# Fewer and wider zero products, one table and one unit's decays moved on GpSimd, weights later on the queue, conversion steps placed by block

## The chip, the core and the metric

The kernel runs on one NeuronCore of a Trainium2 chip. Its engines are PE (TensorE: matrix products, with the weight loads PEld beside them), DVE (VectorE), ACT (ScalarE), POOL (GpSimd) and SP (SyncE, which here issues nearly all DMAs). The metric is the device time of one launch in microseconds.

## What is computed

The reference is retention, followed by two feed-forward blocks, all in float32:

```python
# q, k, v: 8 batches x 8 heads x 576 positions x 64
scores = scale * np.matmul(q, k.transpose(0, 1, 3, 2))
gamma = 1.0 - 2.0 ** (-5.0 - np.arange(H, dtype=np.float32))
Dmat = np.where(rel >= 0, gamma[:, None, None] ** rel[None, :, :], 0.0)   # rel = row - column
attn = np.matmul(scores * Dmat[None, :, :, :], v)
x = attn.transpose(0, 2, 1, 3).reshape(4608, 512)
h = np.maximum(np.maximum(x @ w1, x @ w2), x @ w3)        # 512 -> 768
x = h @ w_out                                             # 768 -> 512
h = x @ w_in                                              # 512 -> 2048
y = (h * np.clip(h + 3.0, 0.0, 6.0) / 6.0) @ w_out2       # 2048 -> 512
```

The weights come as float64 and are turned into float32 on the chip.

## The kernel before

**Units.** One batch and one pair of heads is a unit; there are 32. The first eight (batches 0 and 1, class `Summed`) open the kernel, and the loop over them is written out by hand: what each engine does, and in which order, is the order of the program, and every queue works in that order. A unit's q, k and v ("raw") are loaded by SP in two parts of 576 KB. `prepare` scales k by powers of gamma (on ACT and DVE or POOL for the first four, wholly on POOL for units 4 to 7, L365). `outers` (L382) and `scores` (L284) are its products; `copied` (ACT, L399), `join` (DVE, L416) or `carry` (PE, L405) form the running states; `mask` (DVE, L426) multiplies the scores by a table; `values_mm` (L320) multiplies by v; `values_rest` (DVE, L434) multiplies by a second table and calls `finish`, which splits the result into a high part (ACT, L333) and a low part (L336, a subtraction on POOL or DVE). Every float32 product of the feed-forward parts is three products of such parts: high by high, high by low, low by high (L525, L526, L527). The tables of the four pairs of heads are made by `fill` (DVE, L351). Units 2 to 6 put their subtraction on a list, `low`, that POOL works off from unit 5 on.

**Zeros.** Ahead of the first unit, PE multiplies zeros while the first loads are under way.

**Weights.** The first feed-forward part has 24 tiles of weights. Each goes through the class `Weights`, in the order `order_a`:

- `fetch`: SP loads 512 KB (L100) into one of three buffers `ws`;
- `begin`: two operations on DVE (L113, L114); `rise`: two on ACT (L121, L124);
- `join`: two on DVE (L132, L134), one product on POOL (L136), and then the `fetch` of a further tile, for which SP waits until a buffer is free;
- `end`: the high part by ACT (L147); `lows`: the low part by DVE (L153).

`step` calls, in this order: `end` for the oldest joined tile, `begin`, `rise`, `join` for the oldest tile that had begun before, `lows`. A block calls more steps if its own tile is not ended yet.

**Blocks.** A block (t, f, j) is 12 products: 512 tokens of tile t by weight j (of three) for the hidden slice f; (t, f) alone is the product with the output weights. With j = 0 ACT copies the sum out (L540), with j = 1 and 2 DVE takes the maximum (L542), and with j = 2 the result is split (L53 on ACT, L54 on DVE, the latter by a list that the next block works off). Two PSUM banks serve these sums in turn. Block (0, 0, 0) runs inside the loop, behind unit 6. The rest follows a list, `plan`: slot 0 is (0, 0, 0), slot 1 is (1, 0, 0), slot 2 (0, 0, 1), slot 3 (1, 0, 1), slot 4 (0, 0, 2), slot 5 (1, 0, 2), slot 6 (0, 1, 0) and so on; behind the six blocks of f >= 1 stands the output product (0, f - 1). Behind most slots stands a `step`. Ahead of slot 0's step ACT has `decay(8)`, which scales k of the ninth unit (L261). The ninth and tenth units' loads are issued by SP when the loop over the first eight has ended.

The later units ride along between the blocks, and the second feed-forward part follows; neither is touched.

Of the kernel before, what the change touches and what calls it, by code (L numbers as in the profile page):

```python
# [17 lines left out]
B, H, S, D = 8, 8, 576, 64  # L18
DM, FF1, FF2 = 512, 768, 2048
NT = B * S  # L20
C = 64
NC = S // C
HP = H // 2
KM = DM // P
F1, F2 = FF1 // P, FF2 // P
# [5 lines left out]
NA = 4 * F1  # L31
# [6 lines left out]
def retention_moe_moe2(ctx: ExitStack, tc, raw, w_a, w_b, factors, masks, out):  # L38
    nc = tc.nc
    gamma = [1.0 - 2.0 ** (-5.0 - h) for h in range(H)]  # L40

    def f32(ap):
        return ap.bitcast(F32)
# [28 lines left out]
    def x_tile():  # L72
        return x_pool.tile([P, 2, KM, TB], F32R, tag="x", name="x")

    def acc_tiles():
        return [ps_acc.tile([P, 512], F32, tag=f"o{m}", name=f"o{m}") for m in range(4)]
# [152 lines left out]
    wa = Weights(w_a, order_a, keep, nc.vector)  # L229
# [5 lines left out]
    halves = (slice(0, D), slice(D, P))  # L235

    def load_raw(i, room=None):
        if i >= len(units) or i in raws:
            return
        b, hp = units[i]  # L240
        t = room if room is not None else at.tile([P, RAW], F32, tag="raw", bufs=3, name="raw")
        raws[i] = t

        def part(c0, c1):
            nc.sync.dma_start(out=t[:, c0:c1], in_=raw[b, hp, :, c0:c1])

        if i:
            part(VS1, RAW)
            part(Z0, VS1)
            return  # L250
        part(VS1, VS0)
        part(VS0, RAW)
        part(Z0, VS1)

    def room():
        return rooms.tile([P, RAW], F32, tag="room", bufs=3, name="room")

    def decay(i):
        if i < len(units):
            k = raws[i][:, VS1:VS0]  # L260
            nc.scalar.mul(k, k, kdec_sb[:, units[i][1], NC:])  # L261

    xs, low = {}, []
    banks = [ps_at.tile([P, 512], F32, name=f"at{n}") for n in range(2)]

    class Unit:
# [63 lines left out]
        def finish(self, eng=None):  # L330
            b, hp, y = self.b, self.hp, self.y
            hi, lo = xs[b][:, 0, hp, :], xs[b][:, 1, hp, :]
            nc.scalar.copy(hi, y[:, :TB])  # L333

            def rest(eng):
                eng.tensor_tensor(out=lo, in0=y[:, :TB], in1=f32(hi), op=ALU.subtract)  # L336

            if eng is low:
                low.append(lambda: rest(nc.gpsimd))
            elif eng is not None:  # L340
                rest(eng)
            else:
                late.append(lambda: rest(nc.vector))
                late.append(lambda: nc.sync.dma_start(out=xe_d[:, hp, b * C:(b + 1) * C], in_=y[:, TB:]))
# [3 lines left out]
    def fill(hp):  # L348

        for n, one in enumerate((mask_sb, qdec_sb)):  # L350
            nc.vector.tensor_tensor(  # L351
                out=tables[hp][:, n].rearrange("p (c s) -> p c s", s=C),
                in0=one[:, hp, None, :].to_broadcast([P, NC - 1, C]),
                in1=powers_sb[:, hp, n, :NC - 1, None].to_broadcast([P, NC - 1, C]), op=ALU.mult)

    class Summed(Unit):
# [75 lines left out]
        def values_rest(self):  # L432
            self.y = (rooms if self.hp % 2 else at).tile([P, S], F32, tag="yr", bufs=2, name="yr")
            nc.vector.tensor_tensor(  # L434
                out=self.y[:, :TB], in0=self.ps[1], in1=tables[self.hp][:, 1], op=ALU.mult)
            self.finish(nc.gpsimd if self.i < 2 else low if self.i < 2 * HP - 1 else nc.vector)

        def put_end(self):
            t = raws[self.i].rearrange("p (k s) -> p k s", s=S)
# [91 lines left out]
    def up(t, f, j):  # L531
        x = xs[t]
        ps = ps_mm.tile([P, 512], F32, tag="mm", name="mm")
        for kk in range(KM):
            product(ps, wa_sb[3 * f + j], slice(kk * P, (kk + 1) * P),
                    (x[:, 0, kk, :], x[:, 1, kk, :]), kk == 0, kk == KM - 1)
        flush()
        if j == 0:
            tmp[t, f] = moe.tile([P, TB], F32, tag="t", bufs=3, name="t")
            nc.scalar.copy(tmp[t, f], ps)  # L540
            return
        nc.vector.tensor_tensor(out=tmp[t, f], in0=ps, in1=tmp[t, f], op=ALU.max)  # L542
        if j == 2:
            h = hid[t, f] = moe.tile([P, 2, TB], F32R, tag="hy", bufs=7, name="h")
            split(tmp.pop((t, f)), h[:, 0, :], h[:, 1, :])

    def down(t, f):

        flush()
        if f == 0:  # L550
            acc[t] = acc_tiles()
        h = hid.pop((t, f))
        for m in range(KM):
            product(acc[t][m], wa_sb[3 * F1 + f], slice(m * P, (m + 1) * P),
                    (h[:, 0, :], h[:, 1, :]), f == 0, f == F1 - 1)
            if f == F1 - 1:
                flush()
                if m % 2 == 0:
                    y = f32(pair())
                nc.scalar.copy(y[:, m % 2, :], acc[t][m])  # L560
                if m % 2:
                    late.append(lambda m=m, y=y: nc.sync.dma_start(out=x2_d[t][:, m - 1:m + 1, :], in_=y))
# [10 lines left out]
    with tc.manual_schedule():  # L573

        zeros = stage.tile([P, C], F32, bufs=1, name="zeros")
# [4 lines left out]
        load_raw(1)  # L580
        load_raw(2, room())
        load_raw(3, room())
        wa.fetch(1)
        load_raw(4, room())
        wa.fetch(1)
        load_raw(5)
# [4 lines left out]
        spare = acc_tiles()  # L591
        pairs = [banks, spare[:2], spare[2:],
                 [ps_mm.tile([P, 512], F32, tag="mm", name="mm") for n in range(2)]]
        us = [Summed(i, pairs[i % HP if i < 2 * HP - 1 else 0]) for i in range(2 * HP)]
        for n in range(40):
            nc.tensor.matmul(spare[3][halves[n % 2], :C], lhsT=zeros[halves[n % 2], :], rhs=zeros[halves[n % 2], :],
                             start=True, stop=True)
        us[0].prepare()
        fill(0)
        fill(1)  # L600
        us[0].outers()
        us[0].all_scores()
        us[0].copied(0)
        us[1].prepare()
        us[0].join()
        us[0].mask()
        us[1].outers()
        us[0].values_mm()
        us[1].all_scores()
        us[1].copied(0)  # L610
        fill(2)
        us[2].prepare()
        us[0].values_rest()
        us[1].mask()
        us[1].join()
        fill(3)

        def block(t, f, j=None):

            k = order_a.index(3 * F1 + f if j is None else 3 * f + j)  # L620
            while wa.ended < k + 1:
                wa.step()
            if j is None:
                down(t, f)
            else:
                up(t, f, j)


        for i, u in enumerate(us):
            one, two, three = (us[i + n] if i + n < len(us) else None for n in (1, 2, 3))  # L630
            if i:
                u.values_mm()
            u.put_end()
            if i == 0:
                load_raw(6)
            if i == 2:
                load_raw(7, room())
                wa.fetch(1)
            if one and one.i >= HP:
                one.carry()  # L640
            if three:
                three.prepare()
            if i == 0:
                ends.fill()
            if two:
                two.outers(True)
            if i:
                u.values_rest()
            begun, parts = wa.begun, wa.end() if i in (4, 6) else []
            if 1 < i < 6:  # L650
                wa.begin() if i != 4 else None
                if wa.joined < begun:
                    wa.join()
            wa.lows(parts)
            if two:
                two.copied(0)
                wa.rise()
                two.mask()
                if two.i < HP:
                    two.join()  # L660
            if i >= HP + 1:
                for n in range(2 if i < 2 * HP - 1 else len(low)):
                    low.pop(0)()
            if i == 2 * HP - 2:
                block(0, 0, 0)
        load_raw(8)
        load_raw(9)
        rooms.release()
# [10 lines left out]
        plan += [(0, f, 0), (1, f, 0), (0, f, 1), (1, f, 1), (0, f, 2), (0, f - 1), (0, f), (1, f, 2)]  # L679
        plan += [(1, g) for g in range(f)]  # L680
        decay(2 * HP)
        base = 2 * HP
        side = {(1, 1, 1): [(lambda k: ends.scores(), 0)], (1, 2, 0): [(lambda k: ends.values(), 0)],
                (1, f, 0): [(visit, 0)], (0, f, 1): [(ready, 0)], (1, f, 1): [(rest, 0)]}
        for n, (a, b) in enumerate(zip([(0, f - 1), (1, f, 2), (1, 1), (1, 3)], [(0, f), (1, 0), (1, 2), (1, 4)])):
# [2 lines left out]
        for n, blk in enumerate(plan):  # L688
            if n:
                block(*blk)  # L690
            if wa.ended < NA and n % 3 != 1 and blk != (1, 1, 1):
                wa.step()
                if wa.ended == NA - 1:
                    wb.fetch(2)
            if blk == (0, f, 2):
                xs[2] = x_tile()
            for act, k in side.get(blk, ()):
                act(base + k)
# [325 lines left out]
```

## Time and profile before

| | |
|---|---|
| median of 3 runs | 1457.69 us (1457.62 to 1459.07) |
| profiled execution, its own time | 1459.42 us |
| its span, first to last instruction | 1457.6 us |
| PE busy | 1442.6 us |
| DVE, ACT, POOL busy | 894.7, 448.2, 163.4 us |
[...]

In the rows below, a line of the timeline gives the start and the duration in us, engine, line of the kernel, operation, what it writes and reads, the number of instructions, and in brackets how long the engine was idle before it and who released it. "issue" is a wait for which the profile shows no releaser. A line of the table by stretches gives the stretch, its length, then busy us and instructions of each engine named, the granted clock of PE, the share of the DMA engines and GB/s. In the DMA lists the last number is the time from issue to landing.

### The profile page before, as it was taken

Reading aid. Unit: us, or ns where it says so; the run is one execution under the profiler, and the core shown is the slowest. Engines: PE = TensorE matmul, PEld = TensorE weight load, DVE = VectorE, ACT = ScalarE, POOL = GpSimd, SP = SyncE. Lnnn points to the kernel's source line nnn. Section 1 sums busy time; section 2 is a strip of 40 time slices with the busy share of each in tenths; the row PEclk is TensorE's granted clock in tenths of the full one; section 3 lists DMA queues with packets and bytes.
Section 4 is the critical chain, followed back from the end, with each engine's and each line's share of the span. In section 5 each row is a group of like instructions: output and inputs, shape, how many; then the busy total and the mean of one; then the engine's idle time right before and its main releaser. Section 6 shows DMA issues by size and latency. Waiting matters only on the chain.

```text
span 1457.6 us, 24529 instructions
## 1 busy us (share of the span) xinstructions
PE 1442.6 (99%) x9760; PEld 1248.5 (86%) x9760; DVE 894.7 (61%) x1851; ACT 448.2 (31%) x838; POOL 163.4 (11%) x124
## 2 busy tenths in 40 slices
PE   8999999999999999999999999999999999999998
PEld 7887888888888888888898899899898898898897
DVE  7888878777778752214446646555654655566544
ACT  5544233434343311112222322232232222223222
POOL 4434013333333300000000000000000000000000
PEclk9999999999999999999999999999999999999999
DMA  8434345656565501064643363364445436444431
GB/s 341 155 108 145 134 145 195 224 205 233 198 224 193 199 9 57 2 215 139 224 128 112 117 210 115 101 224 116 116 146 179 116 87 239 116 115 167 116 101 44
DMA packets 94402, 219.02 MB, mean 150 GB/s; under 512 B 14032, under 2 KB 17232, under 8 KB 94288
## 3 DMA queue, kind: packets, MB, share of 16 engines
q1 hardware_dynamic: 93920, 216.96, 45.2%
q8 instruction: 78, 1.28, 0.4%
q10 hardware_dynamic: 368, 0.48, 0.1%
q14 instruction: 36, 0.29, 0.1%
HBM read 174.42 MB, written 42.99 MB: 149 GB/s over the span
## 4 chain that ended last, share of the span: by engine, by line
PE 92%; DVE 5%; ACT 1%; issue 1%; DMA 0%; POOL 0%; ACTq 0%; DVEq 0%; POOLq 0%
PE mm L525 18%; PE mm L527 17%; PE mm L526 17%; PE o L865 5%; PE o L866 5%; PE o L864 5%; PE o L525 3%; PE o L527 3%; PE o L526 3%; PE p L866 3%; PE p L865 3%; PE p L864 3%; PE mm L320 2%; PE at L284 1%; DVE xf L755 1%; DVE g L821 1%
## 5 line engine op out<-in xcount | busy, mean ns | idle before, releaser
L53 ACT CAST gp<-g 128x384 fp32r<-128x384 f32 x192 | 98.6, 513 | 336.5 <-DVE g L821 334.0
L525 PE MATMUL mm<-x,w 128*128 128x512 f32 x468 | 184.6, 394 | 0.1
L527 PE MATMUL mm<-x,w 128*128 128x512 f32 x468 | 182.6, 390 | 0.2
L526 PE MATMUL mm<-x,w 128*128 128x512 f32 x468 | 182.3, 389 | 0.0
L54 DVE TENSOR_TENSOR gp<-g,gp 128x384 fp32r<-128x384 f32 x192 | 107.2, 558 | 112.0 <-ACT gp L53 112.0
L828 DVE TENSOR_TENSOR cc<-mm,c 128x384 f32<-128x384 f32 x142 | 78.7, 554 | 137.2 <-PE mm L527 95.4
L542 DVE TENSOR_TENSOR t<-mm,t 128x512 f32<-128x512 f32 x108 | 74.1, 686 | 136.6 <-PE mm L527 136.5
L865 PE MATMUL o<-w,gp 128*128 128x512 f32 x384 | 151.1, 394 | 0.0
L866 PE MATMUL o<-w,gp 128*128 128x512 f32 x384 | 150.5, 392 | 0.0
L864 PE MATMUL o<-w,gp 128*128 128x512 f32 x384 | 150.1, 391 | 0.0
L525 PE MATMUL mm<-T,wq 128*128 128x384 f32 x382 | 129.6, 339 | 0.9
L833 ACT COPY c<-mm 128x384 f32<-128x384 f32 x143 | 68.5, 479 | 197.1 <-PE mm L527 197.1
L527 PE MATMUL mm<-T,wq 128*128 128x384 f32 x382 | 128.8, 337 | 0.0
L526 PE MATMUL mm<-T,wq 128*128 128x384 f32 x382 | 128.5, 336 | 0.0
L136 POOL TENSOR_TENSOR wf<-wf,wp 128x512 f32<-128x512 f32 x56 | 83.3, 1489 | 317.3 <-DVE wp L134 300.0
L525 PEld LDWEIGHTS mm<-x,w 128*128 128x128 f32 x468 | 87.8, 188 | 19.7 <-DVE t L542 0.5
L527 PEld LDWEIGHTS mm<-x,w 128*128 128x128 f32 x468 | 87.8, 188 | 19.5 <-DVE w L153 1.0
L526 PEld LDWEIGHTS mm<-x,w 128*128 128x128 f32 x468 | 87.9, 188 | 17.9 <-DVE x L336 0.2
L53 ACT CAST h<-t 128x512 fp32r<-128x512 f32 x54 | 33.6, 622 | 205.5 <-DVE t L542 199.9
L525 PE MATMUL mm<-B,wq 128*128 128x384 f32 x286 | 96.4, 337 | 0.0
L527 PE MATMUL mm<-B,wq 128*128 128x384 f32 x286 | 96.3, 337 | 0.0
L526 PE MATMUL mm<-B,wq 128*128 128x384 f32 x286 | 96.1, 336 | 0.0
(182 smaller groups left out, 2917.9 us busy)
## 6 DMA issues: line engine op xcount, KB each, us to landing
wq<-wqd SPq DMA_DIRECT2D x336, 256.0 KB, 3.1
raw<-in_raw SPq DMA_DIRECT2D x55, 576.0 KB, 5.4
ws<-in_w_b SPq DMA_DIRECT2D x32, 512.0 KB, 4.8
ws<-in_w_a SPq DMA_DIRECT2D x24, 512.0 KB, 3.5
wqd<-y SPq DMA_DIRECT2D x24, 512.0 KB, 2.7
x2d<-y SPq DMA_DIRECT2D x18, 512.0 KB, 3.4
wod<-y SPq DMA_DIRECT2D x16, 512.0 KB, 3.2
w<-wod SPq DMA_DIRECT2D x16, 512.0 KB, 4.4
```

The costliest lines, as they stand in the source:

```text
L53: nc.scalar.copy(hi, full)
L54: late.append(lambda: nc.vector.tensor_tensor(out=lo, in0=full, in1=f32(hi), op=ALU.subtract))
L136: nc.gpsimd.tensor_tensor(out=frac, in0=frac, in1=f32(power), op=ALU.mult)
L525: nc.tensor.matmul(ps, lhsT=wh, rhs=xh, start=first, stop=False, skip_group_check=read)
L526: nc.tensor.matmul(ps, lhsT=wh, rhs=xl, start=False, stop=False, skip_group_check=read)
L527: nc.tensor.matmul(ps, lhsT=wl, rhs=xh, start=False, stop=last, skip_group_check=read)
L542: nc.vector.tensor_tensor(out=tmp[t, f], in0=ps, in1=tmp[t, f], op=ALU.max)
L828: nc.vector.tensor_tensor(out=c, in0=a, in1=b, op=ALU.add)
L833: nc.scalar.copy(c, ps)
L864: nc.tensor.matmul(outs[s], lhsT=gh, rhs=wo[f][:, 0, :], start=start, stop=False)
L865: nc.tensor.matmul(outs[s], lhsT=gh, rhs=wo[f][:, 1, :], start=False, stop=False)
L866: nc.tensor.matmul(outs[s], lhsT=gl, rhs=wo[f][:, 0, :], start=False, stop=stop)
```

## The change

1. The zero products become six, each 512 columns wide, instead of forty of 64.
2. `fill` makes the table of the last pair of heads on POOL instead of DVE, and the call moves ahead of unit 0's join.
3. The list `low` goes: units 0 to 6 call their subtraction on POOL at once.
4. One load of weights moves from behind unit 3's load to behind unit 7's; there are again three before the first join.
5. Unit 7's `prepare` moves from the loop's fifth round to its fourth.
6. The steps inside the loop are written out: tile 0 is begun in the fourth round (behind unit 5's mask), joined in the fifth, ended in the sixth, where tile 1 is begun; tile 1 is joined behind block (0, 0, 0).
7. In the plan a step stands behind every block but those of t = 1 with j = 0 or 2, and (1, 1, 1); before, it stood behind two slots of three.

```diff
@@ finish
-            if eng is low:
-                low.append(lambda: rest(nc.gpsimd))
-            elif eng is not None:
+            if eng is not None:
                 rest(eng)
@@ fill
-            nc.vector.tensor_tensor(
+            (nc.vector if hp < HP - 1 else nc.gpsimd).tensor_tensor(
@@ values_rest
-            self.finish(nc.gpsimd if self.i < 2 else low if self.i < 2 * HP - 1 else nc.vector)
+            self.finish(nc.gpsimd if self.i < 2 * HP - 1 else nc.vector)
@@ first loads
         load_raw(3, room())
-        wa.fetch(1)
         load_raw(4, room())
         wa.fetch(1)
         load_raw(5)
@@ zeros
-        for n in range(40):
-            nc.tensor.matmul(spare[3][halves[n % 2], :C], lhsT=zeros[halves[n % 2], :], rhs=zeros[halves[n % 2], :],
-                             start=True, stop=True)
+        for n in range(6):
+            own = halves[n % 2]
+            nc.tensor.matmul(spare[3][own, :].rearrange("p (n d) -> p n d", d=C), lhsT=zeros[own, :],
+                             rhs=zeros[own, None, :].to_broadcast([D, 512 // C, C]), start=True, stop=True)
@@ first units
         us[1].prepare()
+        fill(3)
         us[0].join()
...
         us[1].join()
-        fill(3)
@@ loop over the eight units
                 load_raw(7, room())
-                wa.fetch(1)
+                wa.fetch(2)
...
-            if three:
+            if three and i < HP:
                 three.prepare()
+            if i == HP - 1:
+                us[2 * HP - 1].prepare()
...
-            begun, parts = wa.begun, wa.end() if i in (4, 6) else []
-            if 1 < i < 6:
-                wa.begin() if i != 4 else None
-                if wa.joined < begun:
-                    wa.join()
-            wa.lows(parts)
             if two:
                 two.copied(0)
-                wa.rise()
                 two.mask()
                 if two.i < HP:
                     two.join()
-            if i >= HP + 1:
-                for n in range(2 if i < 2 * HP - 1 else len(low)):
-                    low.pop(0)()
+            if i == HP - 1:
+                wa.begin()
+                wa.rise()
+            if i == HP:
+                wa.join()
+            if i == HP + 1:
+                parts = wa.end()
+                wa.begin()
+                wa.rise()
+                wa.lows(parts)
             if i == 2 * HP - 2:
                 block(0, 0, 0)
+                wa.join()
@@ plan
-        base = 2 * HP
+        base, calm = 2 * HP, [(1, g, j) for g in range(F1) for j in (0, 2)] + [(1, 1, 1)]
...
-            if wa.ended < NA and n % 3 != 1 and blk != (1, 1, 1):
+            if wa.ended < NA and blk not in calm:
                 wa.step()
```

## Rows read from the trace of the kernel before

**Rows 1.** The page, busy time of each engine.

```profile
PE 1442.6 (99%) x9760; PEld 1248.5 (86%) x9760; DVE 894.7 (61%) x1851; ACT 448.2 (31%) x838; POOL 163.4 (11%) x124
```

**Rows 2.** Table by stretches, PE alone (busy us, instructions, clock, DMA share, GB/s).

```profile
5.52:40.66 35.14, 31.04 (x753) 0.95 0.93 362
30.00:35.00 5.00, 4.28 (x81) 0.66 0.45 140
40.66:140.00 99.34, 97.54 (x505) 1.00 0.38 118
```

**Rows 3.** Timeline of PE, 0 to 40 us.

```profile
0.98 3.99 PE L596 MATMUL o<-zeros 64*64 64x64 f32 x80 [0.98 <-DVE rebias L587]
5.52 2.17 PE L382 MATMUL at<-raw 64*64 64x256 f32 x26 [0.55 <-ACT raw L373]
...
24.45 0.27 PE L284 MATMUL at<-room 64*64 64x64 f32 x2 [1.12 <-issue]
...
30.72 1.03 PE L320 MATMUL at<-room 128*64 128x64 f32 x25 [1.90 <-issue]
```

**Rows 4.** The page's DMA queues; table by stretches, PE, PEld, DVE, ACT, POOL.

```profile
q8 instruction: 78, 1.28, 0.4%
...
18.26:24.45 6.19, 4.80 (x127) 3.92 (x127) 5.82 (x12) 2.28 (x5) 3.00 (x3) 1.00 1.02 407
```

**Rows 5.** Timelines of DVE, PE and POOL, 16 to 41 us.

```profile
16.04 1.70 DVE L351 TENSOR_TENSOR w<-masks_sb,factors_sb 128x512 f32<-128x512 f32 x2
...
20.18 1.15 PE L320 MATMUL o<-room 128*64 128x64 f32 x32 [0.28 <-DVE room L416]
...
35.08 5.85 POOL L336 TENSOR_TENSOR x<-yr,x 128x512 fp32r<-128x512 f32 x4
```

**Rows 6.** Timeline of SP, 23 to 38 us; DMA issues, 33.7 to 34.5 us.

```profile
23.43 10.70 SPq L100 DMA_DIRECT2D ws<-in_w_a  x3
34.18 3.51 SPq L245 DMA_DIRECT2D raw<-in_raw  x4
...
ws<-in_w_a SPq DMA_DIRECT2D x1, 512.0 KB, 3.4
...
raw<-in_raw SPq DMA_DIRECT2D x1, 576.0 KB, 4.5
```

**Rows 7.** Timeline of DVE, 39 to 58 us.

```profile
39.82 1.41 DVE L426 TENSOR_TENSOR room<-at,w 64x512 f32<-64x512 f32 x2
41.26 0.69 DVE L434 TENSOR_TENSOR yr<-o,w 128x512 f32<-128x512 f32 x1
...
50.49 0.69 DVE L542 TENSOR_TENSOR t<-mm,t 128x512 f32<-128x512 f32 x1 [1.69 <-PE mm L527]
51.10 0.42 DVE L113 TENSOR_SCALAR wp<-ws 128x512 uint32<-128x512 uint32 x1
...
52.37 0.69 DVE L134 SCALAR_TENSOR_TENSOR wp<-ws,wp 128x512 uint32<-128x512 uint32 x1
52.98 0.68 DVE L153 TENSOR_TENSOR w<-wf,w 128x512 fp32r<-128x512 f32 x1
...
56.56 0.68 DVE L153 TENSOR_TENSOR w<-wf,w 128x512 fp32r<-128x512 f32 x1
```

**Rows 8.** Timeline of ACT, 46 to 56 us.

```profile
46.11 0.77 ACT L261 ACTIVATE raw<-raw,factors_sb 128x576 f32<-128x576 f32 x1
...
54.85 0.62 ACT L147 CAST w<-wf 128x512 fp32r<-128x512 f32 x1 [2.05 <-POOL wf L136]
```

**Rows 9.** Timeline of PE, 47 to 54 us.

```profile
47.55 0.40 PE L525 MATMUL mm<-x,w 128*128 128x512 f32 x1
...
53.71 0.50 PE L527 MATMUL mm<-x,w 128*128 128x512 f32 x1
```

**Rows 10.** Timelines of POOL and PE, 123 to 130 us.

```profile
123.45 4.72 POOL L136 TENSOR_TENSOR wf<-wf,wp 128x512 f32<-128x512 f32 x2 [4.55 <-DVE wp L134]
...
129.24 0.50 PE L525 MATMUL mm<-x,v 128*128 128x512 f32 x1 [1.56 <-ACT t L540]
```

More of the change, by code (lines that the diff above doesn't have):

```diff
@@ L261, in decay @@
             nc.scalar.mul(k, k, kdec_sb[:, units[i][1], NC:])
-    xs, low = {}, []
+    xs = {}
     banks = [ps_at.tile([P, 512], F32, name=f"at{n}") for n in range(2)]
```

## The prediction

> **What bounds the kernel now.** I read the page's busy shares first: PE is busy 99% of the span [rows 1], so only its idle time and its slow clock can be won, and anything that makes it wait is lost in full. Then the busy time of PE by stretches. From the first real product to the first block of the feed-forward part (5.52 to 40.66) it idles 35.14 - 31.04 = 4.1 us, and the mean granted clock is 0.95; from there to 140 us it idles 1.8 of 99 us at full clock [rows 2]. [...] So the stretch that the change touches first holds 4.1 + 1.7 = 5.8 us at most. Third, the timeline of PE: two waits carry the releaser "issue", 1.12 us at 24.45 and 1.90 us at 30.72 [rows 3]: no engine and no data is late there, so the instructions themselves are. The clock falls just behind the second of them. Last, from 40.66 on, the conversion of the weights runs beside the blocks; I read DVE, ScalarE, the issues of SP and their landings there.
>
> **Why instructions are late.** The page's DMA part shows 78 packets of instructions on one queue, 1.28 MB, that is 16.4 KB each; PE and its weight loads record 2 x 9760, some 250 a packet [rows 1, 4]. Between 18.26 and 24.45 stand 127 + 127 records, in 6.2 us with the DMA engines at 1.02 of their time [rows 4], and from 24.45 to the wait that ends at 30.72 it is 6.3 us again [rows 3]. So while the loads fill the queues, PE gets some 256 instructions every 6.2 us.
>
> **The early part of the change.** The 40 small zero products are 80 records and 80 weight loads in 3.99 us [rows 3]; six wide ones are 12 + 12, 136 fewer. Their columns are 6 x 512 = 3072 against 40 x 64 = 2560, so by columns they take 3.99 x 1.2 = 4.8 us, from 0.98 to 5.8, where the first real product stood at 5.52: +0.25 us (ends 0, if the clock rises at the same time and the pairs overlap better, and 0.6). The 136 missing records move every boundary of the instruction packets 136 records further into the work. But each packet is also asked for that much later, 136/254 x 6.2 = 3.3 us, so the pace stays. The packets that came at 18.26 and 24.45 now come at some 21.4 and 27.7 and serve points 136 records on; the third, with the load queue emptying around 31, at some 33.5 instead of 34. Counted off PE's timeline, work alone gets to these points at 20.4, then 25.9 and 32.1, each from the packet before and less the waits of before. That is waits of 1.0, 1.7 and 1.4, 4.1 us. Before lost 1.12 + 1.90, 1.7 by clock [rows 2, 3] and 0.28 to a late join [rows 5]. 4.1 - 5.0 is -0.9, with the zeros **-0.7 us**; ends -5.8 (all of it comes back) and +1.5 (one of the new waits lets the clock fall too).
>
> [...]
>
> The fourth table (fill(3)) leaves DVE, 1.70 us at 16.04, for GpSimd [rows 5]. That brings the mask and join of unit 2 forward, on which PE waited 0.28 us at 20.18 [rows 5]; it is in the walk above. On GpSimd the two products are as wide as its subtractions, of which four took 5.85 us [rows 5]: 2.9 us behind the decays of unit 1, in a stretch where it waits for loads. The subtractions of units 2 to 6 lose their queue "low" and follow their unit; those four ran in a row from 35.08 to 40.93 [rows 5], PE waited for none, and will for none. Unit 7's decays one unit earlier on GpSimd wait for their load with only subtractions behind them; nothing of PE's. These I cost at nothing; their cover is GpSimd's idle time, and if it goes, the first block waits for x.
>
> **Weights later.** One load of weights goes behind unit 4's, one behind unit 7's. The early loads come 512 KB earlier, and go unnoticed by a PE that waits for instructions. What matters is who stands behind the weights on SP. The loads of weights 3 and 4 need the buffers that the joins of weights 0 and 1 free: three such loads took SP from 23.43 to 34.13, and the loads of raw 8 and 9 stand behind them, issued from 34.18 on, right after the second join [rows 6]. **The change moves the join of weight 1 from unit 4 to behind the first block**, and so raw 8 with it. On DVE its two operations (0.69 us each, [rows 7]) now follow, after the masks of unit 7 (1.41), a begin (2 x 0.42), weight 0's subtraction (0.68) and unit 6's product (0.69). The masks could start at 39.1, when PE's scores are there; 39.1 + 1.4 + 0.85 + 0.7 + 0.7 + 1.35 is 44.1. Before, that product ended at 41.95 [rows 7], so the earliest is 43.3; one block by GpSimd makes it 45.4. The next load of weights is issued there, and raw 8 behind it: 34.18 + 4.5 against 33.8, when the weights before it were issued and took 3.4 us to land [rows 6], is 4.9 us to landing. So raw 8 lands at 49.0. ScalarE has its decay (L261, 0.77 us) ahead of weight 1's copy (L147, 0.62) [rows 8]: at 50.4 the copy is done. Block (0,0,1), slot 2 of the plan, wants it at 47.55 [rows 9]: PE waits 2.85 us, and 0.25 more for DVE's subtraction behind the copy. **+3.1 us**, ends 2.1 and 4.4 + 0.25. Everything here is on the clock of before; an earlier PE shifts all of it alike.
>
> **Steps tied to blocks.** I wrote out begin, join and end for each slot, old and new. Before, weight 2 was joined in the step behind slot 0 and ended behind slot 2. Now it is joined behind slot 2 and ended behind slot 3, right ahead of slot 4, block (0,0,2), that needs it. Before ran just these operations at just this place, for weight 3: behind slot 2's maximum (L542 at 50.49) a begin, the join, GpSimd's product, ScalarE's copy at 54.85 to 55.47, and DVE's subtraction at 56.56 to 57.24 [rows 7, 8]. Slot 4's third product, the first to need the subtraction, stood at 53.71, just behind weight 2's subtraction at 52.98 to 53.66 [rows 7, 9]. So weight 2 comes a whole step later: 57.24 - 53.66 = 3.6 us. Slot 2's step has no subtraction of its own any more, which takes some 0.3 off: **+3.3 us** (ends 3.6, and 2.0, where only the copy is late and GpSimd's product isn't held up). What is late next is weight 3 at slot 6, 0.3 us by the same walk, inside these ends; from slot 13 on the new order is level with the old.
>
> **Clock.** In slot 4 PE is idle for some 1.9 us, works on two products, and is idle for 1.5 again. Behind 1.90 us of waiting the clock fell [rows 2, 3]; behind 1.56 us at 129.24 [rows 10] it did not. I take one such fall, **+1.7 us**; ends 0 and 3.4 (slot 2 as well).
>
> **Sum.** -0.7 + 3.1 + 3.3 + 1.7 = +7.4 us. The profiled execution took 1459.42 us with a span of 1457.6, so it would be 1466.8 with a span of 1465.0. Its own time is 1.7 us above the median of the runs, 1457.69; on the median the forecast is **1465.1 us**.
>
> **Rivals.** *Supply comes back whole (faster).* With 136 records fewer and weights out of the queue, packets might be asked for early enough. Then the early 5.8 us and the 0.55 before the first product [rows 3] return, 6.3. It decides from the point where the waits of slots 2 and 4 cost less than 3.4 together (6.3 less the 2.9 of the measurement), that is if one of them is covered; with slot 4 alone at its lower end, 2.0, it is 1457.7 - 6.3 + 2.0 = 1453.4. For it: two "issue" waits lie just at those boundaries. Against: the pace of 6.2 us is the queues', and the order of SP, ScalarE and DVE is fixed by the program. *Even.* Supply gives 5.8 and the waits cost 6.4: 1458.3. *Dearer.* A step behind the last part of the output product and one behind the next (0,f,0) follow without a DVE operation on PSUM between. Before has such a pair once: GpSimd's L136 x2 took 4.72 us from 123.45 while DVE ran on, ScalarE's copy was late, and PE waited 1.56 us at 129.24 [rows 10]. The new order has the pair at slots 12, 19 and 26, two more. With 2 x 1.56 and a second fall of the clock: +4.8, 1469.6. *The early part does nothing*: the waits for instructions end where they ended, whatever the number of records; the early term is 0 and the time 1465.8, inside the forecast.
>
> **How the numbers follow.** The measurement can tell about 0.2%, 2.9 us, from no change. Forecast (1460.6 to 1468.5) 0.52; dearer 0.18; even 0.18; faster 0.12. Below 1454.8 lies the last alone: faster 0.12, same 0.18, slower 0.70. The sum of all low ends is -5.8 + 2.1 + 2.0 = -1.7, that of the high ends 1.5 + 4.65 + 3.6 + 3.4 = +13.2; with the faster case partly inside, the range is 1455.5 to 1471.
>
> **What would show it.** Right: "issue" waits still 6.2 us apart with a full queue; the first raw load of 8 issued behind a join near 44 us; PE waiting for ScalarE's L147 ahead of slot 2 by 2 to 4 us, and at slot 4 for L147 and then L153; half clock behind it. Wrong: no "issue" wait after 20 us and full clock to 40; or slot 2 and 4 starting back to back; then the early term or the order that I wrote out is at fault.

## The result, and the profile after

The changed kernel took 1474.34 us (median of 5 runs, 1473.77 to 1475.43), the kernel before beside it 1459.07 (5 runs, 1457.62 to 1460.03): a ratio of 1.0108, 95% interval 1.0094 to 1.0123. It is slower, as forecast, but by 15 us where 7.4 were forecast: 1474.3 against 1465.1, above the range's end of 1471. The profiled execution took 1475.31 us with a span of 1473.3, which is 15.9 above the profiled execution before.

From 150 us on both traces run alike, so all of it lies ahead of that. The table gives the start of the first product of some slots, before and after; the last column is what was lost since the row above.

| slot | before | after | behind | lost since |
|---|---|---|---|---|
| 0, block (0, 0, 0) | 40.66 | 39.23 | -1.43 | -1.43 |
| 2 | 47.55 | 48.68 | +1.13 | 2.56 |
| 4 | 53.02 | 56.62 | +3.60 | 2.47 |
| 9 | 66.99 | 74.02 | +7.03 | 3.43 |
| 13 | 79.18 | 87.65 | +8.46 | 1.43 |
| 14 | 82.29 | 94.22 | +11.93 | 3.47 |
| 25 | 113.92 | 126.72 | +12.80 | 0.87 |
| 30 | 129.24 | 143.47 | +14.23 | 1.43 |
| 32, and from there on | 134.83 | 150.66 | +15.84 | 1.61 |

At slot 9 the kernel stands where the forecast had it for good, 7.0 against 7.4. Most of what is missing comes behind it, at slots 13 and 30. (The kernel before has 1.56 us of waiting of its own at slot 30, so the last rows show only what the changed kernel adds there.) The timeline of PE, 0 to 144 us, the zeros, the first product and then the lines with the long waits:

```profile
0.98 4.67 PE L594 MATMUL o<-zeros 64*64 64x512 f32 x12 [0.98 <-DVE rebias L584]
5.50 2.17 PE L380 MATMUL at<-raw 64*64 64x256 f32 x26
...
15.92 0.32 PE L380 MATMUL o<-room 64*64 64x128 f32 x1 [0.24 <-issue]
22.24 0.68 PE L320 MATMUL o<-room 128*64 128x64 f32 x15 [1.70 <-issue]
32.84 0.21 PE L284 MATMUL o<-raw 64*64 64x64 f32 x1 [1.25 <-issue]
...
48.68 0.50 PE L523 MATMUL mm<-x,w 128*128 128x512 f32 x1 [1.66 <-ACT w L147]
...
56.62 0.50 PE L523 MATMUL mm<-x,w 128*128 128x512 f32 x1 [1.93 <-ACT w L147]
...
58.39 0.50 PE L525 MATMUL mm<-x,w 128*128 128x512 f32 x1 [1.04 <-DVE w L153]
...
87.65 0.50 PE L523 MATMUL mm<-x,w 128*128 128x512 f32 x1 [0.86 <-ACT w L147]
...
90.33 0.80 PE L525 MATMUL mm<-x,w 128*128 128x512 f32 x1 [1.95 <-DVE w L153]
...
143.47 0.50 PE L523 MATMUL mm<-x,v 128*128 128x512 f32 x1 [2.65 <-ACT t L538]
```

(L523 to L525 are the three products, L525 to L527 before; L538 and L540 are the copy and the maximum, L540 and L542 before.) The first five lines answer to [rows 3], slot 2 to [rows 9], slot 30 to [rows 10]. In the kernel before slots 2, 4 and 13 start without a wait. Here a weight is late at each of them: its high part (L147), and at slots 4 and 13 then its low part (L153) too. The table by stretches (length, then busy us of PE, PEld, DVE, ACT and POOL with instructions, granted clock, DMA share, GB/s) shows what followed:

```profile
5.52:39.23 33.71, 29.66 (x755) 25.64 (x753) 25.23 (x41) 18.93 (x53) 18.71 (x18) 1.00 0.81 317
...
56.62:63.00 6.38, 5.34 (x15) 3.98 (x16) 2.48 (x5) 1.13 (x3) 1.66 (x1) 0.73 0.41 139
...
87.65:94.00 6.35, 4.40 (x12) 3.19 (x13) 5.58 (x10) 1.24 (x2) 2.22 (x2) 0.73 0.30 83
...
143.47:150.00 6.53, 6.53 (x22) 5.23 (x23) 4.55 (x11) 3.25 (x6) 1.27 (x1) 0.74 0.27 84
```

Three times the granted clock fell from 1.00 to 0.50 for part of a stretch (0.50 from 60 to 62, from 91 to 93 and from 145 to 148 us), each time behind waits: (1 - 0.73) x 6.38 = 1.7 us of work at 56.62, 1.7 again at 87.65 and at 143.47. The fall of [rows 2], ahead of 40 us, is not there.

**Slot 2.** The timelines of SP at 42 us and of ACT at 47 us:

```profile
42.21 0.33 SPq L100 DMA_DIRECT2D ws<-in_w_a  x1
42.59 0.42 SPq L245 DMA_DIRECT2D raw<-in_raw  x1
...
47.35 0.77 ACT L261 ACTIVATE raw<-raw,factors_sb 128x576 f32<-128x576 f32 x1 [1.84 <-DMA raw<-in_raw]
48.03 0.60 ACT L147 CAST w<-wf 128x512 fp32r<-128x512 f32 x1
```

The load of raw 8 stands behind the weight that the join of weight 1 let through, ACT's decay waits for it, and the copy of weight 1 stands behind the decay: the chain of the forecast, 1.7 us earlier than reckoned.

**Slot 13.** The timelines of DVE and ACT ahead of it:

```profile
84.05 1.77 DVE L54 TENSOR_TENSOR h<-t,h 128x512 fp32r<-128x512 f32 x1
85.74 0.68 DVE L540 TENSOR_TENSOR t<-mm,t 128x512 f32<-128x512 f32 x1
...
86.45 0.62 ACT L53 CAST h<-t 128x512 fp32r<-128x512 f32 x1 [2.48 <-DVE t L540]
86.98 0.61 ACT L147 CAST w<-wf 128x512 fp32r<-128x512 f32 x1
...
87.11 0.69 DVE L54 TENSOR_TENSOR h<-t,h 128x512 fp32r<-128x512 f32 x1 [0.69 <-ACT h L53]
87.71 0.42 DVE L113 TENSOR_SCALAR wp<-ws 128x512 uint32<-128x512 uint32 x1
...
89.59 0.69 DVE L153 TENSOR_TENSOR w<-wf,w 128x512 fp32r<-128x512 f32 x1
```

Slot 13, block (0, 2, 0), multiplies weight 7, and the new order ends weight 7 in the step behind slot 12, right ahead of it (before, behind slot 11). The copy on ACT waits behind L53 and so for the maximum; on DVE the subtraction (L153) stands last in its step, behind the low part of h (L54) and four operations of two other weights.

**Slot 30.** GpSimd's two products behind slots 26 and 27, from its timeline (this answers to [rows 10], 4.72 us). The first of the two takes 3.47 us; most others in this stretch take 1.6:

```profile
137.69 4.69 POOL L136 TENSOR_TENSOR wf<-wf,wp 128x512 f32<-128x512 f32 x2 [4.55 <-DVE wp L134]
```

### The profile page after: what moved, and what is told of

It reads as the page before. It is cut to its first block, busy times and chain, and to the rows that moved or that the text cites. A ratio compares the mean times of both kernels' runs of the same rounds, so it can differ in the third digit from the quotient of the medians.

```text
span 1473.3 us, 24395 instructions
## 1 busy us (share of the span) xinstructions
PE 1449.0 (98%) x9692; PEld 1248.1 (85%) x9692; DVE 891.7 (61%) x1849; ACT 448.5 (30%) x838; POOL 163.2 (11%) x126
## 4 chain that ended last, share of the span: by engine, by line
PE 89%; DVE 8%; ACT 1%; issue 1%; DMA 1%; POOL 0%; SPq 0%; ACTq 0%; DVEq 0%; POOLq 0%
PE mm L523 17%; PE mm L525 17%; PE mm L524 16%; PE o L866 5%; PE o L867 5%; PE o L865 5%; PE o L523 3%; PE o L524 3%; PE o L525 3%; PE p L867 3%; PE p L865 3%; PE p L866 3%; PE mm L320 2%; PE at L284 1%; DVE xf L756 1%
## 5 line engine op out<-in xcount | busy, mean ns | idle before, releaser
L53 ACT CAST gp<-g 128x384 fp32r<-128x384 f32 x192 | 98.5, 513 | 336.8 <-DVE g L822 334.1
L523 PE MATMUL mm<-x,w 128*128 128x512 f32 x468 | 186.2, 398 | 5.0 <-ACT w L147 4.5
L525 PE MATMUL mm<-x,w 128*128 128x512 f32 x468 | 184.3, 394 | 3.9 <-DVE w L153 3.8
L54 DVE TENSOR_TENSOR gp<-g,gp 128x384 fp32r<-128x384 f32 x192 | 107.2, 558 | 111.8 <-ACT gp L53 111.8
L540 DVE TENSOR_TENSOR t<-mm,t 128x512 f32<-128x512 f32 x108 | 74.1, 686 | 144.6 <-PE mm L525 144.6
L523 PE MATMUL mm<-T,wq 128*128 128x384 f32 x382 | 129.4, 339 | 0.8 <-ACT c L834 0.2
L525 PE MATMUL mm<-T,wq 128*128 128x384 f32 x382 | 128.8, 337 | 0.0
L523 PEld LDWEIGHTS mm<-x,w 128*128 128x128 f32 x468 | 88.5, 189 | 26.0 <-ACT w L147 6.1
L525 PEld LDWEIGHTS mm<-x,w 128*128 128x128 f32 x468 | 88.7, 189 | 25.3 <-DVE w L153 6.5
L53 ACT CAST h<-t 128x512 fp32r<-128x512 f32 x54 | 33.6, 622 | 211.2 <-DVE t L540 198.6
L523 PE MATMUL mm<-B,wq 128*128 128x384 f32 x286 | 96.4, 337 | 0.0
L525 PE MATMUL mm<-B,wq 128*128 128x384 f32 x286 | 96.3, 337 | 0.0
```

Source lines behind the costliest of these rows:

```text
L53: nc.scalar.copy(hi, full)
L54: late.append(lambda: nc.vector.tensor_tensor(out=lo, in0=full, in1=f32(hi), op=ALU.subtract))
L523: nc.tensor.matmul(ps, lhsT=wh, rhs=xh, start=first, stop=False, skip_group_check=read)
L525: nc.tensor.matmul(ps, lhsT=wl, rhs=xh, start=False, stop=last, skip_group_check=read)
```

## The experiments

In each, 1457.9 to 1458.1 us is the median of the kernel before on the same chip, from 13 to 22 runs; "behind" is a start in the profile less that of the profile before. The changed kernel did not run again beside them: where one is said to be less than it, that goes by its 1474.34 us.

**1. The early edits alone** (edits 1 to 5 of the list, the steps as before).

```diff
+            begun, parts = wa.begun, wa.end() if i in (4, 6) else []
... (the steps of the kernel before, in the loop and in the plan)
```

> The kernel before with the early edits alone (zeros, fourth table and subtractions on GpSimd, weights later on SP, unit 7's decays earlier); steps of the conversion as before. Theory A (the early edits help PE's supply of instructions, all the loss is the order of the steps): block (0,0,0) starts near 39.2 us instead of 40.66, no wait above 0.3 us at slots 2, 4 and 13, and the time is 1.4 us under the kernel before. Rival B (the early edits cost, by loads and GpSimd): the time is above the kernel before by 2 us or more.

Measured: 1460.12 us, ratio 1.0013 (1.0003 to 1.0022). Block (0, 0, 0) starts at 42.1, later by 1.4 and not earlier. Timelines of PE, DVE and SP:

```profile
41.53 0.65 PE L403 MATMUL at<-room,factors_sb 64*64 64x256 f32 x4 [0.95 <-ACT room L397]
...
30.87 0.43 DVE L113 TENSOR_SCALAR wp<-ws 128x512 uint32<-128x512 uint32 x1 [2.95 <-DMA ws<-in_w_a]
...
24.34 1.65 SPq L100 DMA_DIRECT2D ws<-in_w_a  x2
```

Weight 1 now comes behind raw 7. The old steps begin it in unit 3, where DVE waits 2.95 us for it, with the mask of the next unit queued behind. Slots 2, 4 and 13 have no wait. So alone the early edits are no gain: the weights come later, and the old steps want them early.

**2. The steps alone** (edits 6 and 7, the early part as before).

```diff
-            begun, parts = wa.begun, wa.end() if i in (4, 6) else []
...
+            if i == HP - 1:
+                wa.begin()
...
-            if wa.ended < NA and n % 3 != 1 and blk != (1, 1, 1):
+            if wa.ended < NA and blk not in calm:
```

> The kernel before with the new order of the steps alone (in the loop and in the plan). Theory A: waits of about 2 us ahead of slot 2, 3 us at slot 4, 2.8 us at slot 13 and 2.7 us at slot 30, the clock falling behind three of them; block (0,0,0) near 40.7 us; 15.7 + 1.4 = 17 us over the kernel before. Rival B: under 10 us over it, since the early edits carry a share.

Measured: 1475.99 us in one run, the whole loss. Block (0, 0, 0) starts at 39.25, as early as in the changed kernel, with the forty small zeros and the waits for instructions of before. Timeline of PE, 24 to 43 us:

```profile
24.16 0.27 PE L284 MATMUL at<-room 64*64 64x64 f32 x2 [0.85 <-issue]
30.43 0.97 PE L320 MATMUL at<-room 128*64 128x64 f32 x25 [1.90 <-issue]
...
42.63 0.50 PE L527 MATMUL mm<-x,w 128*128 128x512 f32 x1 [2.65 <-DVE w L153]
```

So the loss behind 40 us comes with the step order. Slot 4's waits are 1.93 and 1.04, slot 13's 0.87 and 1.94, the same as with all edits. The early start is not shown to come with it: the fall of the clock of [rows 2] is not there in this execution either (23 to 39.25 us at 1.00), and 0.8 of the 1.41 us go with that alone (last section). The 2.65 us in block (0, 0, 0) are 0.47 in the changed kernel, so slot 1 stands 3.1 behind here. Slot 2 then waits 0.36 and not the 2 us expected, slot 30 0.79 and not 2.7. Beside the new steps the early edits seem to pay, by 1.6 us on the whole (1475.99 against 1474.34), but the former is one run.

The size of slot 30's wait is not fixed by the order: with the same steps behind slots 26 and 27, GpSimd's products there were short. Its timeline:

```profile
141.24 1.60 POOL L136 TENSOR_TENSOR wf<-wf,wp 128x512 f32<-128x512 f32 x1 [4.55 <-DVE wp L134]
```

**3. Raw 8 ahead of weight 1's join**, in the changed kernel.

```diff
                 block(0, 0, 0)
+                load_raw(8)
                 wa.join()
```

> The changed kernel with the load of raw 8 issued ahead of the join behind block (0,0,0). If the wait ahead of slot 2 comes from raw 8 standing behind that join on SP (theory A), raw 8 lands by 45 us, ScalarE's decay starts right behind unit 7's copy near 45.5, slot 2 starts without a wait above 0.3 us, and the time falls by 1.9 us; slots 4, 13 and 30 keep their waits. If GpSimd's product of weight 1 is the late one (rival C: it stood behind a subtraction and ended at 44.9), slot 2 still waits 0.5 us or more, and the time falls by under 1 us.

Measured: 1474.57 us in one run. Raw 8 is issued at 36.8, weight 1's copy starts at 45.92, and slot 3 stands 0.5 us ahead of the kernel before instead of 1.5 behind: the cause of slot 2's wait is shown. The 2 us did not stay: 0.8 of them had gone again at slot 5. Timelines of GpSimd and PE further on:

```profile
116.05 4.70 POOL L136 TENSOR_TENSOR wf<-wf,wp 128x512 f32<-128x512 f32 x2 [4.55 <-DVE wp L134]
...
121.85 0.50 PE L523 MATMUL mm<-x,w 128*128 128x512 f32 x1 [2.42 <-ACT t L538]
```

Here the long GpSimd product came up at one place more, behind slots 19 and 20, with 2.42 us of waiting at slot 23.

**4. A step more, behind slot 1**, in the changed kernel: from there on each weight ends one step earlier.

```diff
-... [(1, g, j) for g in range(F1) for j in (0, 2)] + [(1, 1, 1)]
+... [(1, g, j) for g in range(F1) for j in (0, 2) if (g, j) != (0, 0)] + [(1, 1, 1)]
```

> The changed kernel with one step more, behind slot 1, so that each weight is ended one step sooner. Theory A (a weight that is ended in the step right ahead of its slot is late by that whole step): the waits at slot 4 (1.93 + 1.04), slot 9 (0.37) and slot 13 (0.86 + 1.95) go, and with them the two falls of the clock at 59 and 90 us (1.7 each): 9 to 10 us less than the changed kernel. Rival D (DVE and GpSimd have too much to do in this stretch, whatever the order): the waits move to other slots, and under 4 us come back.

Measured: 1464.17 us, ratio 1.0042 (1.0027 to 1.0057), 10.2 less than the changed kernel. The waits of slots 4 and 13 are gone with the clock falls behind them (1.00 from 53.72 to 150 us), so that they come from the place of the steps is shown. The 10.2 agree with the expected 9 to 10 in part by luck: in the profiles some 3.5 us of the difference lie at slots 25 to 32, where slot 30 waits 0.79 here, while a wait at slot 7 and a fall of the clock behind slot 2 (0.50 from 50.31 to 53.72 us) cost 1.5 and some 1.2 us anew. Timeline of PE, what is left of over 1 us:

```profile
48.51 0.50 PE L523 MATMUL mm<-x,w 128*128 128x512 f32 x1 [1.50 <-ACT w L147]
65.72 0.50 PE L523 MATMUL mm<-x,w 128*128 128x512 f32 x1 [1.36 <-DVE t L540]
```

**5. A step more behind slot 11 only**, which leaves slots 2 and 4 as they are.

```diff
-... for j in (0, 2)] + [(1, 1, 1)]
+... for j in (0, 2) if (g, j) != (1, 2)] + [(1, 1, 1)]
```

> The changed kernel with one more conversion step, behind slot 11, so that weight 7 ends there and no longer behind slot 12, right ahead of slot 13 that multiplies it. Slots 2 and 4 are left as they are. Theory: slot 13's 0.86 + 1.95 us of waiting and the half-clock stretch behind them (1.71 us) go; up to slot 12 all is as in the changed kernel, from slot 14 on it stands 7.4 us behind the kernel before instead of 11.9, which is the figure of my forecast for that place; the time falls by 4.5 us to 1469.8 +- 1.2. Rival: the step order as a whole keeps VectorE's chain late, and the wait comes back at one of the slots 14 to 18; the time falls by less than 2 us.

Measured: 1469.6 us (4 runs, 1468.01 to 1474.05), ratio 1.0089 (1.0074 to 1.0105), 4.7 below the changed kernel, as expected, but not in the way expected; one of the four runs is as long as the changed kernel. Timelines of PE, DVE and ACT:

```profile
86.52 0.50 PE L523 MATMUL mm<-x,w 128*128 128x512 f32 x1 [0.87 <-ACT w L147]
87.82 0.50 PE L525 MATMUL mm<-x,w 128*128 128x512 f32 x1 [0.57 <-DVE w L153]
...
82.92 1.77 DVE L54 TENSOR_TENSOR h<-t,h 128x512 fp32r<-128x512 f32 x1
84.62 0.68 DVE L540 TENSOR_TENSOR t<-mm,t 128x512 f32<-128x512 f32 x1
...
85.86 0.61 ACT L147 CAST w<-wf 128x512 fp32r<-128x512 f32 x1
```

The copy's wait at slot 13 is still 0.87: the extra step stands behind slot 11's maximum, which DVE reaches only at 84.62, behind weight 6's subtraction and an L54 of 1.77 us. The subtraction's wait fell from 1.95 to 0.57 and the fall of the clock went (1.00 from 82 to 94 us). From slot 12 to 14 this kernel loses 2.0 us and the changed one 4.9, which is 2.9. The profiled execution, 1468.01, is the shortest of the four, and at slot 32 it stands 7.5 ahead of that of the changed kernel: another 1.1 lie ahead of slot 12 (the clock does not fall behind slot 4 here) and 3.5 at slots 26 to 32. That weight 7's place costs slot 13 the wait for its low part is shown; the wait for the high part goes only where weight 7 ends behind slot 10 (experiment 4). The 4.5 of the expectation are not all its own.

**6. Experiments 3 and 4 together.**

```diff
+                load_raw(8)
                 wa.join()
...
+... [(1, g, j) for g in range(F1) for j in (0, 2) if (g, j) != (0, 0)] + [(1, 1, 1)]
```

> The changed kernel with both mendings: the load of raw 8 put ahead of weight 1's join, and a step behind slot 1 so that each weight ends one step earlier. Theory: the first takes away slot 2's wait of 1.50 us and its half-clock stretch (1.71 us), the second the waits of slots 4 and 13 with theirs; from 1464.2 that leaves 1461.0 +- 1, some 2 to 3 us above before. Rival: what one wait gives back the next late chain takes (as when raw 8 alone was moved: 2 us won at slot 2 and lost again at slot 23); the time stays at 1464 +- 1.

Measured: 1463.11 us, ratio 1.0037 (1.0025 to 1.0049): 1.1 less than with the step alone, not 3: nearer the rival. Slots 2, 4 and 13 have no wait over 0.1; slot 7 has 1.45 and slot 30 has 2.65 again. GpSimd's products at two places, each with DVE's operation beside it, from the timelines:

```profile
106.38 1.61 POOL L136 TENSOR_TENSOR wf<-wf,wp 128x512 f32<-128x512 f32 x1 [4.55 <-DVE wp L134]
106.75 1.51 DVE L113 TENSOR_SCALAR wp<-ws 128x512 uint32<-128x512 uint32 x1
...
126.85 4.69 POOL L136 TENSOR_TENSOR wf<-wf,wp 128x512 f32<-128x512 f32 x2 [4.55 <-DVE wp L134]
127.23 0.42 DVE L113 TENSOR_SCALAR wp<-ws 128x512 uint32<-128x512 uint32 x1
```

**7. The same with the step of slot 27 behind slot 28.**

```diff
-... if (g, j) != (0, 0)] + [(1, 1, 1)]
+... if (g, j) not in ((0, 0), (4, 0))] + [(1, 1, 1), (0, 4, 0)]
```

> The kernel with both mendings, and with the step behind slot 27 moved behind slot 28, so that slots 26 and 27 no longer have one step each. Theory: slot 30's wait (2.65 us there) comes from GpSimd's product that takes 3.47 us beside VectorE's unbroken run of two steps; it goes, nothing later replaces it, and the time falls from 1463.1 to 1460.5 +- 0.8. Rival: the long product comes up at another pair or triple of steps (behind slots 22 to 24 or 29 to 31) and the time stays at 1463 +- 1.

Measured: 1460.6 us, ratio 1.0019 (1.0010 to 1.0029). From the timelines of GpSimd, behind slot 28, and of PE, slot 7:

```profile
128.06 1.61 POOL L136 TENSOR_TENSOR wf<-wf,wp 128x512 f32<-128x512 f32 x1 [4.55 <-DVE wp L134]
...
64.14 0.50 PE L523 MATMUL mm<-x,w 128*128 128x512 f32 x1 [1.41 <-DVE t L540]
```

The long product and slot 30's wait are gone, 2.5 us of the median with them. What still stands against the kernel before, 2.7 us, is slot 7's wait (DVE busy for all of 56.5 to 64.0 with the steps that follow each other there) and 0.74 at slot 23.

**8. In the kernel before, the step of slot 27 behind slot 28.**

```diff
-            if wa.ended < NA and n % 3 != 1 and blk != (1, 1, 1):
+            if wa.ended < NA and (n % 3 != 1 and n != 27 or n == 28) and blk != (1, 1, 1):
```

> Kernel before with the conversion step behind slot 27 moved behind slot 28, so that two steps no longer stand behind neighbouring slots there. Theory: the wait of 1.56 us at 129.24 comes from VectorE's unbroken run of the two steps' operations, beside which GpSimd's product L136 takes 4.72 us instead of 1.4 to 1.7; parted, GpSimd's product takes under 2 us, the wait goes and the time is 1.2 to 1.8 us less (1456.3 against 1458.0). Rival: the wait moves to the next place where VectorE runs unbroken, and the time is within 0.5 us of before.

Measured: 1457.97 us, ratio 0.9996 (0.9987 to 1.0005): no difference that can be told. In its profile the wait of slot 30 [rows 10] is gone and slot 32 stands 1.8 us ahead, yet it is also gone in the profiles of the early edits alone and of the zeros alone, which didn't touch that place. So the kernel before seems to have this wait in some of its executions only: 8 of 22 took over 1459 us, and of the 11 with the step moved none did (1457.25 to 1458.64). Over all three rounds it is 17 of 55, against none of 22 with the step moved (with experiment 11). The median does not move, since most executions are short without the edit too. That the long ones are those with the wait is argued from these times and from two profiles: the one that the forecast rests on (1459.42 us) has it, and so has that of experiment 10 (1459.82 us, 1.58 us at slot 30), where 6 of 10 runs took under 1457.8.

**9. The wide zeros alone**, in the kernel before.

```diff
-        for n in range(40):
+        for n in range(6):
... (each product 512 columns wide, as in the change)
```

> Kernel before with the six wide zero products in place of the 40 small ones and nothing else. Theory: TensorE's instructions arrive in groups of 256, and 34 fewer of them move each border 34 or more instructions on, while the pace of the groups stays; the two waits for nothing shown (1.12 us at 24.45, 1.90 us at 30.72) move later and keep about 3 us between them, so block (0, 0, 0) starts within 0.5 us of 40.66 and the time is within 1.5 us of before. Rival: fewer early instructions bring the later groups sooner; the waits shrink by 1 us or more, block (0, 0, 0) starts by 39.7 and the time falls by about as much.

Measured: 1456.92 us in one run. Block (0, 0, 0) starts at 39.58, and from slot 2 to slot 29 the kernel is 0.7 to 0.8 ahead. Timeline of PE:

```profile
21.92 0.68 PE L320 MATMUL o<-room 128*64 128x64 f32 x15 [1.49 <-issue]
28.13 0.32 PE L382 MATMUL o<-raw 64*64 64x192 f32 x1 [1.21 <-issue]
...
39.00 0.65 PE L405 MATMUL at<-room,factors_sb 64*64 64x256 f32 x4 [0.68 <-ACT room L399]
```

With 0.19 us at 15.81 the waits for instructions are 2.89 us against 3.02: the pace stays at 6.2 us (21.92 to 28.13), as the theory had it; the clock is 1.00 from 5 to 40 us. But block (0, 0, 0) came 1.08 earlier, more than the 0.5 allowed for. The rival had that start (by 39.7), but by shorter waits, which did not come. 0.8 us of it go with the fall of the clock that this execution lacks (last section), so this one run does not show a gain by the zeros.

**10. The early edits with the weights at their old places on the queue**, as experiment 1 but for this:

```diff
         load_raw(3, room())
+        wa.fetch(1)
         load_raw(4, room())
...
                 load_raw(7, room())
-                wa.fetch(2)
+                wa.fetch(1)
```

> The early edits alone (wide zeros, last table and eighth unit's decays on GpSimd, operations of the last units right behind their unit) under the old steps, and with the weights at their old places on SP's queue. Theory: the early edits are worth a little under 1 us by themselves, and lost it when run alone because weight 1 came behind raw 7 (30.8) and VectorE's step stood 2.95 us for it; with the old queue block (0, 0, 0) starts at 39.3 to 40.3 and the time is 0.4 to 1.4 us less than before. Rival: the weights' place is not the cause; block (0, 0, 0) starts at 41.5 or later again, and the time is 1 to 2 us above before.

Measured: 1457.7 us, ratio 1.0003 (0.9994 to 1.0012); block (0, 0, 0) at 40.48. DVE's wait is gone and with it the 1.6 us, so the weights' place was the cause in experiment 1. The gain of 0.4 to 1.4 us is not there: beside the zeros, the other early edits bring nothing that can be told.

**11. The zeros and the moved step, in the kernel before.**

```diff
+        for n in range(6):
...
+            if wa.ended < NA and (n % 3 != 1 and n != 27 or n == 28) and blk != (1, 1, 1):
```

> The kernel before with the two pieces that looked well by themselves: the six wide zero products, and the step of slot 27 behind slot 28. Theory: the zeros are worth 0.7 us from slot 8 on in every execution, and the moved step takes away the wait of slot 30, which the kernel before has in some of its executions only; the median is 0.7 to 1.2 us below before (1457.0 against 1458.05), with no execution over 1458.5. Rival: what block (0, 0, 0) gains is given back at slots 1 to 4, and the median is within 0.3 us of before.

Measured: 1457.19 us (11 runs, 1456.90 to 1457.72), ratio 0.9993 (0.9984 to 1.0002). The median is 0.7 lower and no execution went over 1457.8, but the interval holds 1: no version here is shown to beat the kernel before.

## Why the prediction was right in sign and wrong in size

- **The early part**, forecast -0.7: measured -1.43 at slot 0 and -0.70 at slot 1. The second is the forecast's figure by luck, since the terms behind it came out otherwise. The waits for instructions were reckoned as 1.0, 1.7 and 1.4 at 21.4, 27.7 and 33.5; they are 1.70 at 22.24, none at 27.1 and 1.25 at 32.84, with 0.24 ahead of them at 15.92: 3.2 and not 4.1 us. The borders are where the forecast put them: counting products and weight loads from the start, the waits of both kernels stand ahead of records 450, 706, 962 or 1218, that is 256 or a multiple of it apart. But the pace is not a fixed 6.2 us, since two packets came in the 10.6 us from 22.24 to 32.84.
- **The other early terms.** The zeros took 4.67 us, near the 4.8 reckoned, and yet cost nothing: before, the first product waited 0.55 us for ACT behind them [rows 3], and it stands at 5.50 now and stood at 5.52 then. A rise of the clock during the zeros, with which the low end of that term was put at 0, is not shown: the granted clock is 1.00 from 0 to 5 us, before and after. The fall of the clock was counted as 1.7 us to win, (1 - 0.66) x 5 by [rows 2], and cost 0.8 (last section). And the forecast gave nothing to a loop with fewer conversions in it. From the end of the wait of 1.90 us to block (0, 0, 0) it is 8.82 us with the new steps alone (experiment 2) and 9.13 with the old ones, both at full clock; whether those 0.3 us are the steps' is not shown.
- **Slot 2**, forecast +3.1: the chain is as written, join, load, landing, decay, copy (experiment 3), with raw 8 issued at 42.6 and landed at 47.3 instead of 44.5 and 49.0, since the masks came sooner (at 37.25 instead of 39.1). The load ahead of it was issued at 42.2, where the forecast's earliest was 43.3. It cost 1.8 us from slot 1 to slot 2 and 2.2 to slot 3, so the term was too dear by 0.9.
- **Slot 4**, forecast +3.3 and a fall of the clock, 1.7: measured 1.93 + 1.04 us of waiting and the fall, 4.8 us from slot 3 to slot 7 against 5.0. Up to slot 9 the running total is within 0.4 us of the sum, in part by luck: 0.7 us at slots 8 and 9 (a wait of 0.36 for the low part of weight 4) stand in for what slot 2 did not cost.
- **The step that failed** is the sentence that from slot 13 on the new order is level with the old. The count of ended weights is level only with the step behind slot 13. Behind slot 12 eight have ended and not nine, and the last of the eight is the one that slot 13 needs: weight 7 ends behind slot 12 and no longer behind slot 11, the same case as weight 2 ahead of slot 4. Of the 24 weights these two alone end in the step right ahead of their slot, and before none did. The rule that found slot 4 was not carried down the list to the end. It cost 4.9 us with its fall of the clock (7.03 to 11.93).
- **Clock**, forecast one fall, ends 0 and 3.4: three, 5.1 us, behind the waits at slots 4, 13 and 30, and none behind slot 2's 1.66 (1.00 from 48.68 to 56.62 us). So the two places that the sum left out cost a fall each as well. That is this execution: the same waits at slot 4 in experiment 5 and at slot 30 in experiment 6 brought none (last section).
- **The dearer rival** named the pair of steps at 12, 19 and 26, with 2 x 1.56 more. At 26 the pair cost 2.65 and a fall instead of 1.56, some 3 us over slots 26 to 32. That the pair causes it is shown by experiment 7; its size belongs to the execution, since the same order had 0.79 at slot 30 in experiment 2; at 19 there was 0.57 at slot 23; at 12 it was weight 7. Its time, 1469.6 (by its own terms 1465.1 + 4.8 = 1469.9), was the nearest, for a part of its reason. It also took for a fixed cost what the kernel before seems to pay in some executions only (experiment 8).

## What to carry to other kernels

Where an order of steps is moved, list for every consumer which step ends its input and how many steps lie between, to the end of the list: each place where that distance falls to nothing pays the whole chain, here 3 to 5 us, clock included. Two edits can be cheap together and dear apart: loads moved back are free only if what begins on them moves too. And one profiled execution doesn't tell a wait that is always there from one that comes in some of the executions; look at the spread of the times before putting it into a sum.

## What the runs showed of the hardware

- **Which of the two takes longer where DVE and GpSimd run side by side is not fixed.** In experiment 6 GpSimd's product begins at 106.38, 0.23 us after a DVE subtraction, and at 126.85, 0.22 us after one, with the same operation next on DVE. The first time DVE's L113 takes 1.51 us and the product 1.61; the second time L113 takes 0.42 and the product 3.47. What decides it is not shown.
- **The clock does not fall behind every wait of a size.** In the profile of experiment 8, whose program up to 40 us is that of the kernel before, PE waits as in [rows 3], and the clock stays up. Timeline and table by stretches:

```profile
31.34 0.97 PE L320 MATMUL at<-room 128*64 128x64 f32 x25 [1.90 <-issue]
...
23.00:40.47 17.47, 14.19 (x377) 11.86 (x371) 15.56 (x24) 11.75 (x29) 11.01 (x10) 1.00 0.82 310
```

  Later waits show the same. Experiment 5 has the 1.93 and 1.04 us of waiting at slot 4 and experiment 6 the 2.65 at slot 30 (PE waits there until 132.64), and their stretches, here with PE's clock third from the end, stay at 1.00, where the changed kernel fell to 0.73 and 0.74:

```profile
56.50:60.00 3.50, 2.25 (x9) 1.56 (x10) 1.92 (x4) 1.30 (x3) 1.67 (x1) 1.00 0.58 198
60.00:64.00 4.00, 4.00 (x19) 3.17 (x17) 2.91 (x6) 2.19 (x4) 0.21 (x1) 1.00 0.18 70
...
120.00:150.00 30.00, 27.30 (x165) 21.82 (x167) 22.75 (x37) 12.67 (x24) 11.14 (x6) 1.00 0.39 128
```

  In experiment 8, from the end of the wait at 31.34 to block (0, 0, 0), at 40.47, it is 9.13 us, and 9.94 in the profile before, with the fall: the 1.7 us of slow work of [rows 2] cost 0.8 on the path. A wait of 0.26 us for ACT at 39.89 comes up instead. So the forecast counted as winnable what another engine's chain held back in part.
